# Reordering the logits' copy, the early gathers' operands and the early tile's transposes at the end of a fused attention and mixture-of-experts kernel

## The chip, the cores and the metric

The kernel runs on one core of a Trainium2 chip. The metric is the time of one execution on the device, in microseconds (us), as the median of several runs; lower is better. A core has five engines that work side by side, each through its own queue of instructions: TensorE (matrix products; PE in the profile, and PEld for its weight loads), VectorE (DVE), ScalarE (ACT), GpSimd (POOL) and SyncE (SP, which here only starts transfers). They meet through semaphores.

## What is computed

The reference is windowed attention, followed by a layer in which every token goes to one of eight experts. Shapes: 4 sequences of 768 tokens, 8 heads of width 64, 8 global columns, a local window of 96; 3072 tokens of width 512, experts 512 to 1024 to 512.

```python
scores = scale * np.matmul(q, k.transpose(0, 1, 3, 2)) + bias   # bias: -slope of the head * distance
scores = np.where(is_global | is_local, scores, -1000000000.0)
a = softmax(scores)
x = (a @ v) as tokens x 512

logits = x @ w_gate
expert_idx = np.argmax(logits, axis=1)
gate_w = softmax(logits)[own expert]
for e in range(E):
    xe = x[expert_idx == e]
    out[expert_idx == e] = gate_w * (np.maximum(xe @ w1[e], 0.0) @ w2[e])
```

## The kernel before, in words

**Attention.** A block is 128 queries of one sequence: 24 blocks, six in each of the four sequences. The loop in `banded` (L475 to L528) has steps n = 0 to 24, and in step n it works on several blocks at once, one stage each. All orders are those in which the code is written: the engines' queues are filled in program order (`manual_schedule`), nothing is moved by a scheduler. For the middle steps the order is:

- `scores(n)`: 32 products into two PSUM tiles `sp` (L360); VectorE adds the bias into two tiles `p` (L374, or L371 for a sequence's first block).
- `prep_q(n + 1)` and `prep_k(n + 1)`: transposes of the next raw q and k (L237), copied by ScalarE (L242); GpSimd puts the global columns into `ka` (L296, L297).
- `both(n - 1)`: VectorE adds the two halves of p of the block before into `pb` (L390), which gives the softmax sums.
- `exps(n, ...)`: the first of two exponentials on ScalarE (L381).
- `tokens(n - 2)`: TensorE transposes the router's row `rs` (L428) and the attention output `ot` (L431, into `px`); ScalarE copies the logits from PSUM to `part` (L436); VectorE forms the softmax denominators (L439, L441), the logits (L444, L447) and the scaled rows of x (L450, `xr`). For the last block of a sequence `choose` (L170 to L178) picks the expert, and in a later step `gates` (L181 to L190) forms the gate values.
- `values(n - 1)`: probabilities times v (L402) into `po`, copied by ScalarE into `ot` in two halves (L406); then the router's row into the PSUM tile `pr`: softmax sums (L413) and logits (L417), copied by ScalarE into `rs` (L420). `pr` has one buffer, which is free again once `part` is copied.
- the second exponential of block n, and `mix_v` (L281, GpSimd).

In steps 8, 14 and 20 a finished sequence is dispatched: `dispatch` counts places by small products (L198, L202), VectorE turns them into row numbers (L205 to L212), and in the steps that follow GpSimd scatters the rows of x to `xs_dram`, two blocks a step (L215).

**The early tile.** After three sequences the first 128 tokens of experts 0 and 1 are known. `early()` computes their row numbers by eight VectorE operations (L777 to L790) and gathers them (L732); `x_in_s(0)` transposes the first tile (L797), VectorE copies it (L798) and sets targets and gates (L799, L801). Its up-projection (`up_s`, L806) is the first work of the experts, and covers the dispatch of the fourth sequence. In step 24 the order is scores' sums `both(23)`, `values(23)`, `tokens(22)`, the early tile's `x_in_s(0)`, and after the loop `tokens(23)`.

**Experts.** `passes` then goes through all eight experts, by a scheme with seven products for eight (L978, L1040, L1049) and smaller forms for the rest of an expert's tokens; the change leaves it alone.

## Time and profile before

| | us |
|---|---|
| median of three runs (517.68, 518.26, 724.41) | 518.26 |
| profiled execution, span | 515.9 |
| attention up to the first up-projection (L806 in the chain) | 164.15 |
| TensorE busy | 498.8 |
| VectorE busy | 316.8 |
| ScalarE busy | 162.3 |
| GpSimd busy | 190.5 |

The granted TensorE clock is 0.997 over the span. A profile is one execution. Each row of a timeline gives the start, the busy time, the engine, the line and the operation with the tile written and the tiles read; in square brackets stands the idle time of the engine before it, and after the arrow who ended that wait. An engine that isn't the bottleneck may stand idle without cost, so the table's shares say little by themselves: what counts is which engine the others wait for in the stage that is changed. In the middle of attention the chain of waits goes through TensorE for step after step:

```profile
97.38 1.99 PE sp L360 x32
99.36 1.02 PE pt L237 x8
100.93 1.90 PE po L402 x32
103.25 0.52 PE pr L413 x10
104.35 1.99 PE sp L360 x32
```

One step takes some 7 us here, from scores to scores (97.38 to 104.35).

### The profile page before, as it was taken

To read this page: it belongs to the slowest core of one execution; us is meant where nothing else is said; L and a number is where in the kernel's file an instruction comes from. 1 tells how busy PE (TensorE), PEld (TensorE's weight loads), DVE (VectorE), ACT (ScalarE), POOL (GpSimd) and SP (SyncE) were. 2 spreads that over 40 slices of the span, in tenths; PEclk is the share of its full clock that TensorE was granted. 3 is DMA by queue.
4 is the path that set the end of the run, shared out by engine and by line. 5 is a ranking of instruction groups with operands and counts; after the bars stand their busy time and mean duration, and the time that the engine had idled before them with its cause. 6 is when DMAs were issued, how large, how long until landed. Compare 5 with 4: busy or idle time off the path is not lost.

```text
span 515.9 us, 12427 instructions
## 1 busy us (share of the span) xinstructions
PE 498.8 (97%) x5019; PEld 422.2 (82%) x5019; DVE 316.8 (61%) x666; ACT 162.3 (31%) x346; POOL 190.5 (37%) x285
## 2 busy tenths in 40 slices
PE   7999999999997999999999999999999999999994
PEld 4888888888886679679799788869969868896983
DVE  4787977977977646528599068128527705822741
ACT  4666656656652002113112012103102212211120
POOL 5431251351442573334384065034316305502503
PEclk9999999999999999999999999999999999999998
DMA  9999789789921321064191461047264108400101
GB/s 183 210 236 222 174 231 226 182 216 230 317 84 44 124 76 61 8 240 184 26 386 52 164 246 39 1 146 287 74 218 166 26 1 291 151 2 23 44 4 50
DMA packets 96334, 72.77 MB, mean 141 GB/s; under 512 B 79324, under 2 KB 79326, under 8 KB 96228
## 3 DMA queue, kind: packets, MB, share of 16 engines
q1 hardware_dynamic: 87808, 52.44, 36.8%
q0 software_dynamic: 7872, 19.01, 10.6%
q8 instruction: 54, 0.88, 0.8%
q14 instruction: 52, 0.43, 0.3%
q10 hardware_dynamic: 548, 0.02, 0.1%
HBM read 61.46 MB, written 14.73 MB: 148 GB/s over the span
## 4 chain that ended last, share of the span: by engine, by line
PE 86%; issue 5%; DVE 5%; DMA 1%; SPq 1%; POOL 1%; ACT 1%; POOLq 0%; ACTq 0%
PE u L978 18%; PE u L806 10%; PE d L1040 9%; PE sp L360 8%; PE d L1049 7%; PE u L816 7%; PE po L402 6%; PE pt L237 4%; PE d L816 3%; PE pr L413 3%; PE u L1147 3%; PE u L1122 3%; DVE p L374 2%; PE t L958 2%; PE px L431 1%
## 5 line engine op out<-in xcount | busy, mean ns | idle before, releaser
L1056 DVE TENSOR_TENSOR UV<-UV,d 128x512 f32<-128x512 f32 x8 | 5.5, 688 | 110.9 <-ACT yu L1150 81.3
L740 POOL DMA_INDIRECT out_dram<-ys,to_u x8 | 8.3, 1041 | 142.6 <-ACT yu L1150 87.6
L374 DVE TENSOR_TENSOR p<-sp,other 128x1024 f32<-128x1024 f32 x40 | 47.2, 1219 | 18.0 <-PE sp L360 13.8
L806 PEld LDWEIGHTS u<-xsT,w 128*128 128x128 f32 x448 | 50.9, 192 | 2.9 <-issue 2.0
L806 PE MATMUL u<-xsT,w 128*128 128x128 f32 x448 | 51.8, 276 | 0.9 <-DVE gates L801 0.9
L978 PE MATMUL u<-cx,c 128*128 128x128 f32 x384 | 48.1, 275 | 0.0
L381 ACT ACTIVATE p<-p 128x1024 f32<-128x1024 f32 (+1 forms) x48 | 47.2, 987 | 1.8 <-DVE p L374 1.6
L978 PEld LDWEIGHTS u<-cx,c 128*128 128x128 f32 x384 | 45.5, 192 | 0.0
L402 PE MATMUL po<-p,vt 128*64 128x128 f32 x704 | 43.7, 276 | 0.8 <-issue 0.5
L402 PEld LDWEIGHTS po<-p,vt 128*64 128x64 f32 x704 | 38.1, 137 | 5.0 <-issue 3.9
L978 PE MATMUL u<-xT,w 128*128 128x128 f32 x256 | 39.6, 277 | 0.0
L360 PE MATMUL sp<-qt,kt 64*128 64x128 f32 x448 | 37.8, 276 | 0.6 <-DVE kt L244 0.6
L816 PE MATMUL u<-w,huT 128*128 128x512 f32 x80 | 35.1, 592 | 0.0
L978 PEld LDWEIGHTS u<-xT,w 128*128 128x128 f32 x256 | 34.2, 192 | 1.0 <-issue 0.2
L360 PEld LDWEIGHTS sp<-qt,kt 64*128 64x128 f32 x448 | 31.0, 188 | 2.4 <-issue 1.2
L1040 PE MATMUL d<-c,ch 128*128 128x256 f32 x128 | 32.8, 379 | 0.0
L296 POOL COPY ka<-kt 128x384 f32<-128x384 f32 x16 | 10.1, 634 | 56.7 <-ACT kt L242 56.7
L215 POOL DMA_INDIRECT xs_dram<-xr,slot_i x24 | 24.4, 1016 | 16.2 <-DVE cnt L868 7.5
L816 PEld LDWEIGHTS u<-w,huT 128*128 128x128 f32 x80 | 15.2, 190 | 17.0 <-issue 16.7
L1005 ACT COPY uv<-u 128x256 f32<-128x256 f32 x32 | 11.9, 371 | 51.2 <-PE u L978 42.1
L390 DVE TENSOR_TENSOR pb<-p 128x512 f32<-128x512 f32 x40 | 27.6, 731 | 0.0
L1040 PEld LDWEIGHTS d<-c,ch 128*128 128x128 f32 x128 | 24.3, 190 | 3.3
(256 smaller groups left out, 1044.7 us busy)
## 6 DMA issues: line engine op xcount, KB each, us to landing
w<-in_moe_w_dram SPq DMA_DIRECT2D x24, 1024.0 KB
w<-in_moe_w_dram SPq DMA_DIRECT2D x16, 512.0 KB
raw_q<-in_q_dram SPq DMA_DIRECT2D x24, 256.0 KB
raw_k<-in_k_dram SPq DMA_DIRECT2D x24, 256.0 KB
vt<-in_v_dram SPq DMA_DIRECT2D x24, 256.0 KB
xs_dram<-xr,slot_i POOLq DMA_INDIRECT x24
xg<-xs_dram,grow POOLq DMA_INDIRECT x16
mu<-xs_dram,grow_e POOLq DMA_INDIRECT x16
```

The source lines that it names most:

```text
L215: d = nc.gpsimd.indirect_dma_start(out=xs_dram[:], out_offset=bass.IndirectOffsetOnAxis(ap=slot_i[:, u:u + 1], axis=0), in_=xr[:, u, :].bi ...
L237: nc.tensor.transpose(pt[:, m, :], src[:, 2 * m:2 * m + 2, :].rearrange("p a d -> p (a d)"), ident[:])
L360: nc.tensor.matmul(sp[:, a, j, t, :], lhsT=kt[r, m, :], rhs=qts[n][r, m, :], start=True, stop=True, skip_group_check=True)
L374: nc.vector.tensor_tensor(z, sc, bi, ALU.add)
L381: nc.scalar.activation(z, z, AF.Exp)
L390: nc.vector.tensor_tensor(t[:].rearrange("p a j c -> p (a j) c"), z[:, :, 0, :], z[:, :, 1, :], ALU.add)
L402: nc.tensor.matmul(po[D * a:D * a + D, m % 2, :], lhsT=vt[:, 2 * m + a, :], rhs=ps[n][m // 2][:, a, m % 2, t, :], start=(x == 0), stop=(x ...
L806: nc.tensor.matmul(ph[:, i, :], lhsT=self.w[e % 2][0][:, c, ts(half * HF + i, P)], rhs=xT[:, c, :], start=(c == 0), stop=(c == NDC - 1), s ...
L816: nc.tensor.matmul(py[:].rearrange("p a b -> p (a b)"), lhsT=h[:, f, :], rhs=self.w[e % 2][1][:, f, :], start=(f == 0), stop=(f == NFC - 1 ...
L978: nc.tensor.matmul(bank[:, r, :], lhsT=lhs(k), rhs=rhs(k), start=first, stop=True, skip_group_check=True)
L1040: nc.tensor.matmul(self.half(i, j), lhsT=lhs, rhs=rhs, start=(f == 0 and j == 0), stop=True, skip_group_check=True)
L1049: nc.tensor.matmul(self.half(i, j), lhsT=lhs(f), rhs=rhs(f), start=False, stop=True, skip_group_check=True)
```

## The change

Four lines of the loop move, and one function is cut in two.

- The first exponential of step n (for 1 < n < 24) goes behind `tokens(n - 2)`, so that ScalarE's queue has the copy of the logits (L436) ahead of it. For step 0 nothing changes.
- `early()` keeps its eight VectorE operations and goes from step 23 to step 22, behind the last scatters; its two gathers become `gather_early()`, in step 23.
- In step 24 the early tile's `x_in_s(0)` goes ahead of `tokens(22)`.

The aim is that VectorE gets the logits earlier in each step, that GpSimd need not wait for the gathers' operands, and that the first up-projection need not wait for work on the last tokens.

```diff
-            if n < N and n != 1:
-                exps(n, slice(0, 1 if 0 < n < N - 1 else 2))
             if n == 0:
+                exps(n, slice(0, 2))
                 biases(1, (0, 1, 2, 3), "act")
...
             if n == N:
                 rs[n - 1] = values(n - 1)
+                ex.x_in_s(0, ps_t.tile([P, NPAIR, P], F32, tag="t", name="pt"))
             if n >= 2:
                 tokens(n - 2, rs.pop(n - 2))
...
+            if 1 < n < N:
+                exps(n, slice(0, 1 if n < N - 1 else 2))
             if 0 < n < N:
                 rs[n - 1] = values(n - 1)
             if 0 < n < N - 1:
                 exps(n, slice(n != 1, 2))
-            if n == N:
-                ex.x_in_s(0, ps_t.tile([P, NPAIR, P], F32, tag="t", name="pt"))
             if n < N:
                 mix_v(n)
             if i == 2 and b == B - 1:
                 send()
+                ex.early()
             if i == 3 and b == B - 1:
-                ex.early()
+                ex.gather_early()
...
             nc.vector.tensor_scalar(self.inv_s[:, 0:NS], inv[:], float(2 ** 30), None, MUL)
-            for e in range(NS):
-                self.gather(self.xs[:, e, :], self.grow_s[:, e:e + 1])
             shape = [P, E, 5]
...
+        def gather_early(self):
+            for e in range(NS):
+                self.gather(self.xs[:, e, :], self.grow_s[:, e:e + 1])
```

## The prediction

> **What bounds the kernel now.** I read the busy shares first, then busy time by stage, the waits, the three timelines of the last attention steps, and the chain that ended last. The page's first two parts:

> ```profile
> PE 498.8 (97%) x5019; PEld 422.2 (82%) x5019; DVE 316.8 (61%) x666; ACT 162.3 (31%) x346; POOL 190.5 (37%) x285
> PE   7999999999997999999999999999999999999994
> ```

> TensorE is busy nearly all the time, with one dent: the thirteenth slice, around 155 us, the end of attention. A saving must be time in which TensorE stands still, and it must lie before about 164 us. The busy times by stage (columns: window, length, busy us of each engine) price that dent:

> ```profile
> 10.00:30.00 20.00, 19.94 (x306) 17.03 (x306) 14.86 (x33) 14.59 (x30) 11.86 (x27) 1.00 1.12 213
> 150.00:165.00 15.00, 11.09 (x166) 9.18 (x165) 11.01 (x32) 5.75 (x13) 4.93 (x6) 1.00 0.21 73
> 165.00:208.00 43.00, 42.78 (x296) 34.71 (x295) 27.52 (x83) 6.34 (x14) 22.88 (x28) 1.00 0.24 78
> ```

> From 150 to 165 us TensorE lacks 3.9 us; from 10 to 150 us it lacks 2.6 us in all (140 less the 137.4 us that the stages sum to). After 165 us it lacks next to nothing, so whatever is gained before stays gained. About 6.5 us is the most that this region can give. The waits between 149.5 and 164.2 us (engine and line, who was waited for, total, times, longest) say who takes it:

> ```profile
> POOL xs L732 <- DVE loc L788: 3.6, 1, 3.6
> PE pr L413 <- ACT part L436: 1.7, 1, 1.7
> PE u L806 <- DVE gates L801: 0.9, 1, 0.9
> PE pr L413 <- DVE pb L390: 0.7, 2, 0.5
> PE pt L797 <- DMA xs<-xs_dram,grow_s: 0.7, 1, 0.7
> ```

> The change speaks to each: L436 is the copied logits, L788 the last of the early operands, L797 the early tile's transposes. But a wait names who came last, not who comes next once it is gone. So the ScalarE timeline of step 23 and the chain (time, length, what):

> ```profile
> 153.45 2.19 ACT L381 ACTIVATE p<-p 128x1024 f32<-128x1024 f32 x2 [1.56 <-DVE p L374]
> 155.54 0.25 ACT L436 COPY part<-pr 128x128 f32<-128x128 f32 x1
> 155.69 0.65 ACT L406 COPY ot<-po 128x256 f32<-128x256 f32 x2
> ```

> ```profile
> 152.13 2.36 DVE p L374 x2
> 154.48 1.50 DVE pb L390 x2
> ...
> 157.47 0.08 DVE cnt_s L777
> ...
> 158.60 1.22 DVE pb L390 x2
> 159.82 0.04 issue
> 159.86 0.52 PE pr L413 x10
> ...
> 163.40 0.60 DVE xsT L798
> ```

> The part copy sits behind both exponentials, but so do the two ot copies, which the same router product needs at L417. And from 152 to 160 us the chain runs almost wholly on VectorE: score sums, pb sums, the tokens' rows, the eight operations of early() (157.4 to 158.6 us), then the pb sums of the last block. VectorE bounds this end, not the 1.7 us ScalarE wait.

> [...] the logits of step 23 are in PSUM at 151.82 us, yet their copy starts at 155.54. [...] the first early gather is an instruction of 1.09 us at 158.47, while TensorE's transposes of what it brings are let go at 162.06, 3.6 us after its start. [...] the pair of pb sums takes 1.28 us alone and 1.59 with GpSimd copies beside it (132.95 us). The change moves two gathers, so I allow 0.3 us for that.

> **The change, part by part.**

> (a) *Part copy ahead of the first exponential, in the steps whose router product waits for it.* In steps 7, 13 and 19 (52.03, 89.82, 128.14 us) TensorE waits 0.33 us for the copy, 1.0 in sum. The copy's input is there earlier: in step 19 its transpose is done by 126.4 (0.11 us at 126.24 in the chain), and ScalarE's kt copy ends at 126.99. So it runs at 126.9 instead of 127.83. But ScalarE does the same sum of work, so the ot copies still end at 128.6; L417's last four matmuls follow at 128.6 and the next scores at 128.85, against 129.03. I take 0.17 of each 0.33: 3 x 0.17 = **0.5 us** (bounds 0.2 and 1.0). In all other steps the copy is hidden behind TensorE's matmuls, and the exponential is 0.15 us later (the start-to-start of copy and next copy, 155.54 to 155.69), which the values of the *next* step do not feel: its product is wanted some 5 us later. Nothing there.

> (b) *The same, seen by VectorE.* In those three steps VectorE stands 1.40 us for the copy (den at 52.01, 89.80 and 128.12). With the copy ready at 127.15 the tokens' rows and the choice of expert end 0.97 us earlier, and the next score sums, now without any gap behind them at 130.68, start when their own scores allow: 128.85 + 1.17 (16 score matmuls) + 0.04 = 130.06, 0.62 earlier. Behind them in VectorE's queue are pb, tokens, dispatch and the next pair, an unbroken run up to 141.93 us, where TensorE waits for pb (0.40 us as matmul, 0.67 with its weight load, at 141.98). That run comes 0.62 earlier, 0.45 beyond what (a) already gave. In steps 9 and 15 the same wait is 0.29 and 0.34 us as a weight load (65.41, 103.25), of which I take 0.3 each. Sum 0.45 + 0.3 + 0.3 = **1.05 us** (bounds 0.4 and 2.0, the latter if the 0.3 us waits for ot in those steps shrink too).

> (c) *The 1.68 us wait of step 23.* Copy done at 152.1, so the product may start at 154.16. It can't: pb of block 22 ends its halves at about 155.1 and 155.99, and the ot copies now start at 155.54 instead of 155.69. Its matmuls end at 156.7, not 156.82: **0.1 us** (bounds 0 and 0.3). Two waits take the removed one's place.

> (d) *The eight operations of early() a step ahead.* In step 23 they occupy 157.38 to 158.52, 1.14 us of VectorE on the chain. In step 22 they fall between 150.57 (the end of the tokens' rows) and 152.13, where VectorE stands 1.56 us: hidden by that wait. So the last pb sums run 157.4 to 158.7, the last values end at about 158.65, and the router product ends at 159.6 instead of 160.71: 1.1 us, of which (c) gave 0.1. **1.0 us** (bounds 0.6 and 1.3).

> (e) *Gathers and the early tile.* The gathers' operands no longer hold GpSimd (3.63 us). They follow the vt copy (154.24 to 154.84) and start at 154.9; the same 3.6 us put the first tile in place at 158.5, over a microsecond before its transposes. These now follow the product at 159.6: 0.44 us of matmul, 0.2 to the copy, 0.60 copy, 0.15 for tos and gates: up-projection free at 161.2, and the tokens' transposes (0.55 + 0.55 us) fill TensorE meanwhile. Before: product end 160.71 to up-projection 164.15 is 3.44 us; after, 159.6 to 161.25 is 1.65. That is 1.8 us; it contains the gather wait (0.65) and the gates wait (0.91). Against it stands a debt: the last tokens' VectorE work follows the early tile's, and the expert choice ends at 161.1 + 1.57 (161.83 to 163.40) + 2.16 (164.05 to 166.21) = 164.85, while the dispatch comes up at 161.25 + 3.53 (164.15 to 167.68) = 164.8. The slack of 1.5 us (166.21 to 167.68) is used up. [...] **1.4 us** (bounds 0.5 and 2.0).

> After that GpSimd's scatters come 0.7 us nearer to TensorE than before; the tile they lead to was fetched from 181 us and is wanted at 189.97, so that is hidden.

> Sum: 0.5 + 1.05 + 0.1 + 1.0 + 1.4 = 4.05 us. 518.26 - 4.05 = 514.2 us, 0.8% less.

> **Rivals.** *Handed on:* VectorE or the engines' handshakes take back most of it. For it: some score sums wait until well after their scores (in step 22, at 145.12, 1.2 us after the first 16 matmuls), all in steps where scatters are under way, and gathers now move beside the last products. Then (a) at 0.2, (b) 0.4, (d) 0.6, (e) 0.5: 1.7, or 516.6 us. *All waits go:* every TensorE wait listed above and 1.0 in steps 7, 13, 19, 0.67 in 21 and 0.6 in 9 and 15 vanish: 1.7 + 0.9 + 0.7 + 0.7 + 1.0 + 0.67 + 0.6 = 6.3, or 512.0 us. Against it: the ot copies behind the exponentials. *Slower:* the copy ahead holds up the exponentials where TensorE waits for them next; 0.27 us (a whole copy) in each of some 20 steps costs 5.4 us, less (d), (e) at their low 1.1: 522.6 us. Against it: no TensorE wait in the trace names an exponential (L381).

> **How the numbers follow.** Forecast 0.60, handed on 0.25, all waits 0.10, slower 0.05. 514.2 us is the likeliest case. The range 511.8 to 517.2 us takes in the lower bounds of the terms' sum (1.7 us), the all-waits case, and leaves out the slower case and a little on each side. Over 2% would be 10.4 us either way, more than the 6.5 us that TensorE stands idle in this region and more than the slower case: faster 0.02, within 0.95, slower 0.03.

> **What would show it.** (a) L413 no longer waits for L436 anywhere; the 0.33 us waits shrink by half, with ot in their place. (b) At the step-21 dispatch L413 no longer waits for pb. (c) In step 23 L413 waits for pb instead. (d) L777 lies near 149 us and the last pb pair starts some 1.1 us sooner after the first. (e) GpSimd's gathers start before 155 us, and the first up-projection follows the last router product by under 2 us. I am wrong if the exponentials appear as a releaser of TensorE, if the dispatch waits for the expert choice by more than half a microsecond, or if the part after the first up-projection changes its length.

## The result and the profile after

The changed kernel takes 514.61 us in the median of six runs (514.32 to 514.86); the kernel before, run beside it, 517.68 in the median of five (517.00 to 518.26). A sixth run of the kernel before took 724.41 us and is left out. The ratio is **0.9941, with a 95% interval of 0.9927 to 0.9955**: a gain of 3.1 us, 0.6%. That is less than 2%, but well outside the scatter of the runs. The prediction said 514.2 us and a range of 511.8 to 517.2. The time came out closer than the gain: the sum said 4.05 us, and started from 518.26.

The first two parts of the page of the changed kernel, busy time by engine and the slices of TensorE:

```profile
PE 499.4 (97%) x5019; PEld 422.4 (82%) x5019; DVE 318.4 (62%) x666; ACT 162.3 (32%) x346; POOL 192.3 (38%) x285
PE   8999999999999999999999999999999999999994
```

The work is the same, and the dent in the thirteenth slice is gone. Busy times by stage, changed kernel, same columns as before:

```profile
10.00:150.00 140.00, 139.01 (x2162) 121.03 (x2159) 115.55 (x251) 89.11 (x185) 52.47 (x87) 1.00 0.87 216
150.00:165.00 15.00, 13.53 (x185) 11.94 (x182) 12.39 (x39) 6.17 (x14) 4.15 (x5) 1.00 0.20 62
```

TensorE lacked 3.9 us between 150 and 165 us; now it lacks 1.5. From 10 to 150 us it lacked 2.6 and now lacks 1.0. The windows stand still while the work moves, so the gain is better counted between events:

| from … to | before, us | after, us | gain, us |
|---|---|---|---|
| scores of block 1 … scores of block 23 | 10.98 … 149.51 | 10.58 … 148.22 | 0.89 |
| scores of block 23 … first up-projection | … 164.15 | … 160.10 | 2.76 |
| first up-projection … first product of the eight experts (L978, L981 after) | 30.13 long | 30.59 long | −0.46 |

The sum, 3.19 us, is close to the 3.1 us of the ratio. (The two profiled spans, 515.9 and 512.5 us, differ by 3.4: the scores of block 1 come 0.40 us earlier, and what follows the last row of the table is 0.2 us longer.) The waits of TensorE between 148 and 161 us, where there had been four, and further on one that the prediction did not have:

```profile
PE pr L413 <- DVE pb L390: 1.4, 1, 1.4
...
PE d L819 <- DVE loc L910: 0.6, 1, 0.6
```

The waits for the logits' copy, for the gates and for the gather are gone. The first remaining line is step 23, where pb has taken the place of the copy; the second is the down-projection, at 172.3 us. ScalarE's timeline of step 23, changed kernel (start, length, what):

```profile
151.16 0.27 ACT L436 COPY part<-pr 128x128 f32<-128x128 f32 x1 [0.54 <-PE px L431]
152.28 2.19 ACT L381 ACTIVATE p<-p 128x1024 f32<-128x1024 f32 x2 [0.86 <-DVE p L374]
154.38 0.63 ACT L406 COPY ot<-po 128x256 f32<-128x256 f32 x2
```

The copy is now ahead of both exponentials, but the two ot copies still follow them. The chain that ended last, from step 23 to the first up-projection (start, length, what):

```profile
150.97 2.36 DVE p L374 x2
153.32 1.38 DVE pb L390 x2
...
154.75 0.52 PE pr L413 x10
...
158.51 0.59 PE pt L800 x4
...
160.19 3.76 PE u L809 x32
```

Before, the chain ran on VectorE up to 159.82 us, through the eight operations of early() and a second pair of pb sums. Now it leaves VectorE at 154.70 and stays on TensorE, with the early tile's transposes (L800) directly behind the last router product.

One thing about these two profiles has to be known for what follows. In both, VectorE starts the score sums of step 23 late: 2.62 us after the scores before the change, 2.75 after it. In seven of the eight profiles from two other chips, used in the experiments, it is 1.21 us (1.52 in the eighth), and there the changed kernel has no wait for pb in step 23 at all: the router product follows the value products at once, and TensorE waits 0.62 us for the early gather instead. There is no profile of the kernel before from those two chips, so how its time divides there is not known.

### The profile page after: what moved, and what is told of

It is laid out like the page before. It is cut to its first block, busy times and chain, and to the rows that moved or that the text cites. A ratio compares the mean times of both kernels' runs of the same rounds, so it can differ in the third digit from the quotient of the medians.

```text
span 512.5 us, 12427 instructions
## 1 busy us (share of the span) xinstructions
PE 499.4 (97%) x5019; PEld 422.4 (82%) x5019; DVE 318.4 (62%) x666; ACT 162.3 (32%) x346; POOL 192.3 (38%) x285
## 4 chain that ended last, share of the span: by engine, by line
PE 85%; DVE 7%; issue 5%; DMA 1%; SPq 1%; POOL 1%; POOLq 0%; ACT 0%; DVEq 0%
PE u L981 18%; PE u L809 10%; PE d L1043 10%; PE sp L360 8%; PE d L1052 7%; PE u L819 7%; PE po L402 6%; PE pt L237 3%; DVE p L374 3%; PE pr L413 3%; PE u L1150 3%; PE u L1125 3%; PE d L819 2%; DVE pb L390 2%; PE t L961 2%
## 5 line engine op out<-in xcount | busy, mean ns | idle before, releaser
L374 DVE TENSOR_TENSOR p<-sp,other 128x1024 f32<-128x1024 f32 x40 | 47.1, 1218 | 19.2 <-PE sp L360 14.2
L981 PE MATMUL u<-cx,c 128*128 128x128 f32 x384 | 48.1, 275 | 0.0
L381 ACT ACTIVATE p<-p 128x1024 f32<-128x1024 f32 (+1 forms) x48 | 47.7, 997 | 1.1 <-DVE p L374 0.9
L981 PEld LDWEIGHTS u<-cx,c 128*128 128x128 f32 x384 | 45.5, 192 | 0.0
L981 PE MATMUL u<-xT,w 128*128 128x128 f32 x256 | 39.6, 277 | 0.0
L981 PEld LDWEIGHTS u<-xT,w 128*128 128x128 f32 x256 | 34.2, 192 | 1.1 <-DVE cx L974 0.2
L390 DVE TENSOR_TENSOR pb<-p 128x512 f32<-128x512 f32 x40 | 28.3, 748 | 0.0
## 6 DMA issues: line engine op xcount, KB each, us to landing
w<-in_moe_w_dram SPq DMA_DIRECT2D x16, 512.0 KB
```

The lines of the kernel that those rows point to most:

```text
L374: nc.vector.tensor_tensor(z, sc, bi, ALU.add)
L381: nc.scalar.activation(z, z, AF.Exp)
L390: nc.vector.tensor_tensor(t[:].rearrange("p a j c -> p (a j) c"), z[:, :, 0, :], z[:, :, 1, :], ALU.add)
L981: nc.tensor.matmul(bank[:, r, :], lhsT=lhs(k), rhs=rhs(k), start=first, stop=True, skip_group_check=True)
```

## The experiments

My theory: the gain is made at the end of attention, by gathers that start early and a tile that no longer stands behind the last tokens; the first move, of the logits' copy, gives a little in the steps around each dispatch. Rivals: each move brings its own share whatever the others do; the gain is all in the first move; the ot copies hide more than I had thought. Three groups of runs, each on a chip of its own, with the kernel before beside it: its medians were 517.69, 514.21 and 514.33 us. The first group is the single moves and the run without the first move; the third starts with "The changed kernel again". So I compare ratios, or kernels of one group. "Over the changed kernel" on the first two chips means against 0.9941 of the kernel before there; on the third the changed kernel ran itself. A step's length is counted from its scores to the next block's.

### One move alone

**The logits' copy alone** (the first exponential behind `tokens(n - 2)`, the rest as before):

```diff
-            if n < N and n != 1:
-                exps(n, slice(0, 1 if 0 < n < N - 1 else 2))
             if n == 0:
+                exps(n, slice(0, 2))
...
+            if 1 < n < N:
+                exps(n, slice(0, 1 if n < N - 1 else 2))
```

> Only the first move: the logits' copy ahead of the exponentials; early operands, gathers and the early tile stay as in the kernel before. My theory (terms a, b, c): VectorE gets the logits earlier, the wait for pb in the dispatch steps goes, and in step 23 pb takes the copy's place: 0.9 us less than before (517.0), most of it in steps 9 to 21, and no gain between the scores of block 23 and the first up-projection. Rival (ScalarE wait is the bound at the end): step 23 gives its 1.7 us too, 2.6 us less (515.3). Rival (all handed on): no change (517.9).

517.13 us, ratio 0.9989 (0.9982 to 0.9995): 0.56 us gained. Steps 9, 15 and 21 take 6.34, 6.53 and 6.75 us, where the kernel before takes 6.94, 6.97 and 7.12. From the scores of block 23 to the first up-projection it takes 14.66 us, as before (14.64): nothing at the end. Both are as my theory had it.

**The operands alone** (`ex.early()` in step 22, `ex.gather_early()` in step 23, the gathers cut out of `early`):

```diff
+                ex.early()
             if i == 3 and b == B - 1:
-                ex.early()
+                ex.gather_early()
```

> Only the second move: the eight operations of early() in step 22, the gathers alone in step 23. My theory (term d and the gather wait of e): VectorE's chain in step 23 is 1.1 us shorter and the gather's 0.65 us wait goes, but the early tile's copy stays behind tokens(22) on VectorE: 1.4 us less than before (516.5). Rival (the operands only cost GpSimd idle time): 0.65 us or less (517.3).

516.62 us, ratio 0.9975 (0.9967 to 0.9984): 1.3 us. The end takes 13.20 us, 1.44 shorter. TensorE now waits 1.2 us for the gates, 0.9 before: the gathers land early, but the tile stands behind the last tokens.

**The early tile alone** (`x_in_s(0)` ahead of `tokens(22)`):

```diff
             if n == N:
                 rs[n - 1] = values(n - 1)
+                ex.x_in_s(0, ps_t.tile([P, NPAIR, P], F32, tag="t", name="pt"))
...
-            if n == N:
-                ex.x_in_s(0, ps_t.tile([P, NPAIR, P], F32, tag="t", name="pt"))
```

> Only the third move: the early tile's transposes ahead of tokens(22). My theory: the gather still lands at about 162 us, so TensorE waits there with the tokens' transposes behind it; up-projection 0.4 us earlier, but the last tokens' VectorE work and the expert table later, so that TensorE waits longer for the table's forms: between 0.5 us less and 0.5 us more, 517.9 within noise. Rival (the gates wait of 0.91 us is removed by this move alone): 0.9 us less (517.0).

517.8 us, ratio 1.0001 (0.9991 to 1.0011). TensorE's waits between 146 and 168 us in this kernel:

```profile
PE pr L413 <- ACT part L436: 1.8, 1, 1.8
PE pt L796 <- DMA xs<-xs_dram,grow_s: 1.3, 1, 1.3
```

The gates' wait is gone, and the wait for the gather has grown from 0.7 to 1.3 us: one took most of the other's place. The first up-projection still comes 0.49 us earlier (14.15 us after the scores of block 23), but from there to the first product of the eight experts it takes 30.60 us, not 30.13: TensorE stands 0.66 us in the down-projection, where it stood 0.22. So what was won was lost there, as the theory in that text had it.

The three moves alone give 0.56 + 1.3 + 0 = 1.9 us, together 3.1. Each of these is known to 0.3 to 0.7 us only, but the traces say the same: between the scores of block 23 and the first up-projection the single moves take off 0, 1.44 and 0.49 us, together 2.76. So they need one another.

### One move undone

**Without the first move** (changed kernel, first exponential back in its old place):

```diff
+            if n < N and n != 1:
+                exps(n, slice(0, 1 if 0 < n < N - 1 else 2))
             if n == 0:
-                exps(n, slice(0, 2))
```

> The second and third move without the first. My theory: the end of attention gains as in the changed kernel, 2.7 us from the scores of block 23 to the first up-projection, less 0.4 us at the table's forms: 2.3 us less than before (515.6), 1.0 us over the changed kernel. If the first move does nothing: as the changed kernel (514.6). If the first move is needed for the end (the 1.7 us wait comes back): 1.7 us or more over the changed kernel (516.3).

516.29 us, ratio 0.9969 (0.9958 to 0.9981): 1.45 us over the changed kernel by the ratios, 1.65 by the medians (0.9941 of 517.69 us is 514.64). That lies between the 1.0 of my theory and the 1.7 of the last case, and it came by a way that none of them named. TensorE's timeline at the end (start, length, what, idle time before it):

```profile
155.31 0.70 PE L413 MATMUL pr<-pb,one_in 128*32 128x128 f32 x16 [1.82 <-DVE pb L390]
...
156.20 3.55 PE L402 MATMUL po<-p,vt 128*64 128x128 f32 x32
```

The last 32 value products take 3.55 us; in this kernel's other steps they take 1.97. The busy times by stage show why; the column ahead of the DMA share is the granted clock:

```profile
153.00:156.00 3.00, 1.18 (x34) 0.94 (x30) 2.93 (x6) 2.73 (x5) 1.90 (x3) 1.00 0.01 3
...
157.00:158.00 1.00, 1.00 (x12) 1.00 (x11) 1.00 (x3) 0.27 (x1) 0.98 (x2) 0.50 0.79 173
```

In the three microseconds up to 156 TensorE worked for 1.18; then the clock fell (0.69, 0.50, 0.50 and 0.61 in the four microseconds from 156 to 160; it is full again behind them), which cost 3.55 − 1.97 = 1.6 us. The profiles of the kernels before and after hold the full clock there, with gaps of 1.68 and 1.37 us.

The fall did not come in every run of this kernel. The mean granted clock of a run is on record: of the eight, five have 0.994, as the profiled one (516.22 to 517.38 us), and three 0.997 to 0.998 (515.22, 515.31 and 516.32 us). All profiles with no fall have 0.996 to 0.999. The three lie, by their median, 0.7 us over the changed kernel; the rest of the 1.65 us goes with the fall.

**Without the second move** (`ex.early()` whole, with its gathers, in step 23):

```diff
-                ex.early()
             if i == 3 and b == B - 1:
-                ex.gather_early()
+                ex.early()
```

> The changed kernel with the second move undone: early() whole in step 23 again. My theory (term d and the gather): its eight operations lie on VectorE's chain again (1.1 us) and the gather lands when the early tile is wanted, so the first up-projection comes 2 to 2.5 us later than in the changed kernel: 516.9. Rival (the first move alone carries the end): within 0.5 us of the changed kernel (515).

513.17 us, ratio 0.9982 (0.9972 to 0.9991): 0.0041 of 514.21, 2.1 us over the changed kernel. The end takes 12.56 us against 10.79 in the changed kernel on the third chip (1.8 longer), and TensorE waits 1.3 us for the early tile's gather again, the same as with the early tile alone. Three of the ten runs, at 513.87 to 514.00 us, have the mean clock of 0.994 that goes with a fall; the profiled one has none.

**Without the third move** (`x_in_s(0)` back behind `values`, the rest changed):

```diff
-                ex.x_in_s(0, ps_t.tile([P, NPAIR, P], F32, tag="t", name="pt"))
...
+            if n == N:
+                ex.x_in_s(0, ps_t.tile([P, NPAIR, P], F32, tag="t", name="pt"))
```

> The changed kernel with the third move undone: the early tile behind tokens(22) again. My theory (term e without the gather): its copy waits behind 1.5 us of tokens(22) on VectorE, so the up-projection is 1.2 us later, but TensorE does not wait longer for the expert table's forms (0.4 us): 0.8 us over the changed kernel, 515.4. Rival (additive with the single moves, where the tile alone gave nothing): as the changed kernel, 514.6. Rival (gates wait of 0.91 and idle TensorE bring the slower clock back, as in the run without the first move): 516.4.

511.66 us, ratio 0.9948 (0.9934 to 0.9961): 0.36 us over the changed kernel, half of what I expected, and by the intervals not to be told from it. In the profiles the first up-projection is indeed 0.75 us later (11.53 us after the scores of block 23, against 10.79), with 1.3 us of waiting for the gates. But further on:

```profile
PE d L820 <- issue: 0.2, 1, 0.2
```

The down-projection stands only 0.2 us, where the changed kernel's stands 0.65, and the stretch from the first up-projection to the eight experts takes 30.12 us, not 30.59. So of the 0.75 us that the third move wins ahead of the up-projection 0.47 is lost here. The run with the forms' table read later comes back to it.

### What holds the rest

**The ot copies ahead of the first exponential**, in steps 2 to 22 (changed kernel otherwise):

```diff
-        def values(n):
+        def values(n, mid=None):
...
+            if mid:
+                mid()
...
-            if 1 < n < N:
-                exps(n, slice(0, 1 if n < N - 1 else 2))
+            if n == N - 1:
+                exps(n, slice(0, 2))
             if 0 < n < N:
-                rs[n - 1] = values(n - 1)
+                rs[n - 1] = values(n - 1, (lambda: exps(n, slice(0, 1))) if 1 < n < N - 1 else None)
```

`mid` runs between the ot copies and the router product.

> The changed kernel with the two copies of the attention output also ahead of the first exponential (steps 2 to 22). My theory (term c and the failed term a: the ot copies took the place of the logits' copy): the 0.3 us wait for ot in steps 7, 13 and 19 goes, and those in steps 9 and 15: 1.0 us under the changed kernel, 513.6. Rival (VectorE's pb sums come last in those steps): no change, 514.6. Rival (the exponential now comes too late for the next values): slower, 516 or more.

511.11 us, ratio 0.9938 (0.9924 to 0.9952), 0.2 us under the changed kernel by the ratios, and not to be told from it, as the first rival has it. The steps tell more. Step 19 of the kernel before, from the second ot copy to the next scores (start, length, what):

```profile
127.97 0.67 ACT L406 COPY ot<-po 128x256 f32<-128x256 f32 x2
...
129.03 0.49 PE L360 MATMUL sp<-qt,ka 64*128 64x128 f32 x4
```

The same of the changed kernel:

```profile
127.04 0.66 ACT L406 COPY ot<-po 128x256 f32<-128x256 f32 x2
...
127.47 0.42 PEld L417 LDWEIGHTS pr<-ot,gate_w 128*32 128x32 f32 x8 [0.29 <-ACT ot L406]
...
128.09 0.49 PE L360 MATMUL sp<-qt,ka 64*128 64x128 f32 x4
```

and of this kernel (the lines of the file are two further on):

```profile
125.28 0.75 ACT L406 COPY ot<-po 128x256 f32<-128x256 f32 x2 [0.33 <-PE po L402]
...
125.90 0.33 PEld L419 LDWEIGHTS pr<-ot,gate_w 128*32 128x32 f32 x8
```

With the ot copies ahead, L419 has no wait, and steps 7, 13 and 19 fall from 5.87 to 5.47 us each. So it was the ot copies that held them at 5.87 after the logits' copy had been taken away. But steps 9, 15 and 21 go from 6.34, 6.53 and 6.75 us (changed kernel, third chip) to 6.67, 6.67 and 7.06. Step 21 of this kernel shows who holds it:

```profile
139.31 0.52 PE L415 MATMUL pr<-pb,one_in 128*32 128x128 f32 x10 [0.40 <-DVE pb L390]
```

No exponential is named there. From the logits of step 19 to the pb sums of step 21 VectorE works with no gap over 0.1 us and ends them 18.3 us after the scores of step 19, as in the changed kernel (18.4). TensorE now gets there 0.4 us earlier, and waits. So of the 1.2 us that was won 0.8 is handed back, by VectorE's unbroken run.

**The forms' table read later** (changed kernel, one line moved):

```diff
         ex.down_s(0, ex.hsT, 0, ex.d[0])
-        ex.load_forms()
         ex.down_s(0, ex.hsT, 1, ex.d[0])
+        ex.load_forms()
```

`load_forms` reads a form for each expert from a small table into the engines' registers, TensorE's too; VectorE writes the table in `table()`.

> The changed kernel with TensorE's reading of the expert forms one group of eight products later, behind the first early tile's second half. My theory (the debt of the third move: VectorE's table comes nearer to TensorE, which waits for it at 172.3 us): the gap of 0.77 us in the down products goes: 513.9. Rival (the reading itself costs TensorE's queue a microsecond wherever it stands): no change, 514.6.

510.3 us, ratio 0.9923 (0.991 to 0.9937): 0.9 us under the changed kernel by the ratios, whose intervals overlap. In the profile the first up-projection comes 29.70 us ahead of the first product of the eight experts, where the changed kernel has 30.59: the same 0.9 us, and the rival fails. The timelines around 170 us (start, length, what, idle time before it): first the kernel before, then the changed one with the table's last write, then this one:

```profile
175.88 2.38 PE L816 MATMUL d<-w,hsT 128*128 128x512 f32 x5 [0.22 <-issue]
```

```profile
170.89 0.17 DVE L898 TENSOR_SCALAR form<-k_i 128x8 int32<-128x8 int32 x1
...
172.30 1.96 PE L819 MATMUL d<-w,hsT 128*128 128x512 f32 x4 [0.65 <-DVE loc L910]
```

```profile
165.03 7.03 PE L819 MATMUL d<-w,hsT 128*128 128x512 f32 x16
```

Half of the sixteen products lie ahead of the read and half behind it. In the first two kernels TensorE stands between the halves, 0.22 and 0.65 us; with the read eight products later the sixteen products are one run. The wait's name, L910, was only the VectorE instruction that ended last before it; what TensorE's queue waited for is the read of the table, whose last write, at L898, ends 1.2 us before the next product. All the profiles agree: with the third move and the read in its old place the gap is 0.53 to 0.66 us (eight kernels), without the third move 0.21 to 0.22 (four).

**The changed kernel again**, beside the next three:

> The changed kernel once more, beside the three that follow. Expected: 0.994 of the kernel before. In steps 7, 13 and 19 a period of 5.87 us from scores to scores, as before the change; at the table's forms a wait of 0.65 us. If the late score sums of steps 10, 11 and 22 belong to the change: periods of 6.8 to 7.1 us there; if to the chip: on one where they are missing 6.34 us, as in the runs e5 to e8.

511.25 us, ratio 0.9941 (0.9928 to 0.9955), the same ratio as at first. The end takes 10.79 us, and steps 10, 11 and 22 take 6.34 us each, where the first profile of this kernel has 6.81, 7.13 and 6.78; the wait at the forms is 0.65 us in both. So the late score sums go with the chip. The changed order has a part in where they fall: in the first group step 10 is long only in the kernels with the first move (6.81 and 6.84 us), step 16 only in those without it (6.91 to 6.97; 6.50 in the one with the clock's fall).

**Both together**, ot copies ahead and the table read later:

> The changed kernel with both: ot copies ahead of the first exponential, and the forms read one group later. My theory: 0.4 us in each of steps 7, 13 and 19, of which steps 9, 15 and 21 take back 0.8 because VectorE's pb sums come last there, and 0.65 us at the forms: 1.0 us under the changed kernel run beside it, 0.992 of the kernel before. Rival (the two are the same slack seen twice): 0.65 us under it.

510.26 us, ratio 0.9919 (0.9905 to 0.9932): 1.0 us under the changed kernel beside it and 4.1 under the kernel before. The runs alone do not tell 1.0 from the rival's 0.65. But both savings are in the profile, each in its place: the sixteen products are one run, and steps 7, 13 and 19 take 5.47 us. It is the fastest of the versions tried on that chip.

**The scatters spread**, one a step instead of two in the first two sequences, to see whether they make some score sums late:

```diff
-            for _ in range(min(2, len(sends))):
+            for _ in range(min(2 if n >= 20 else 1, len(sends))):
```

> The changed kernel with the scatters of the first two dispatched sequences one a step over six steps, instead of two a step over three. Theory (score sums start late while scatters are in flight): on a chip where steps 10, 11 show it, the lateness shrinks there and shows in later steps; the total within 0.5 us of the changed kernel. Rival (lateness has nothing to do with scatters): the same periods in steps 10 and 11. On a chip without the lateness: no change beyond 0.3 us.

522.13 us, ratio 1.0158 (1.0144 to 1.0172): slower, and for a reason that I had missed. VectorE's wait:

```profile
DVE xr L450 <- DMA xs_dram<-xr,slot_i: 10.4, 2, 6.8
```

The rows of the next sequence overwrite a buffer that is still being scattered, so step 15 takes 10.16 and step 21 13.58 us. On this chip no score sums were late in the first place, so the run says nothing on its question.

**Idle products in the gap, without the first move**: the kernel without the first move, with six matmuls that add nothing to the result ahead of step 23's router product, to keep the clock up:

```diff
+        def fill():
+            t = ps_s.tile([P, 2, 2, 2, P], F32, tag="s", name="fill")
+            spot = t[:, 0].rearrange("p j t c -> p (j t c)")
+            for _ in range(6):
+                nc.tensor.matmul(spot, lhsT=idle[:, 0:P], rhs=idle[:], start=True, stop=True,
+                                 skip_group_check=True)
...
-                rs[n - 1] = values(n - 1)
+                rs[n - 1] = values(n - 1, fill if n == N - 1 else None)
```

> The second and third move without the first, with six idle products on zeros (about 1.3 us at full clock) in TensorE's gap of step 23, so that it does not stand still there. They add no work to the result. Theory (the 1.8 us gap brought the half clock that cost 1.6 us in the run without the first move): no stretch of clock under 1.0 around 157 us, and 0.7 us over the changed kernel run beside it. Rival (the slower values of block 23 had another cause): 1.7 us over it. Rival (the idle products push the router product back): 1 us or more over it with full clock.

512.34 us, ratio 0.9964 (0.995 to 0.9977): 1.1 us over the changed kernel beside it. The clock is full around 157 us, and no run has a mean under 0.996, so this is the worth of the first move with no fall of the clock in it. 0.9 of it is in steps 9, 15 and 21 (6.67, 6.72, 7.12 us without the move; 6.34, 6.53, 6.75 with it), nothing in steps 7, 13 and 19 (5.87 in both). The end is 0.35 us longer (11.14 against 10.79), so the idle products can account for about that much at most, not for the 1 us of the last rival. Whether they kept the clock up is not shown: the kernel without them did not run on this chip.

## Why the prediction was right, and where it was not

The direction, the time and the place were right: 3.1 us measured against 4.05 summed, most of it at the end of attention. The gain was a quarter too large; that the time still came within 0.4 us of 514.2 is luck, since the sum started from 518.26 and the kernel before took 517.68 beside the changed one. By its own steps:

**(a) Steps 7, 13, 19: predicted 0.5, measured 0.** These steps take 5.87 us each, before and after. The wait for L436 is gone, as said, but the ot copies took all of it, not half. The step that failed is "L417's last four matmuls follow at 128.6 and the next scores at 128.85": it lets the scores start 0.25 us after the ot copies. In both traces it is 0.39 (128.64 to 129.03 before, 127.70 to 128.09 after). So the next scores had followed the ot copies all along; the wait for the logits' copy ran beside theirs, and taking it away could give nothing. The run with the ot copies ahead shows it: without them in the way 0.4 us falls from each step.

**(b) The pb waits of steps 9, 15, 21: predicted 1.05, measured 0.9 to 1.4.** The mechanism is as forecast. VectorE stands 0.45 us for the copy in step 19, not 1.40, and the score sums of step 20 start 7.08 us after the scores of step 19, not 7.52: 0.44 earlier, where the prediction had 0.45 beyond what (a) gives. The wait of 0.40 us at the step-21 dispatch is gone from the list. By the idle-product run the three steps give 0.9 us; by the two profiles of before and after 0.61 + 0.44 + 0.37 = 1.4. In those two profiles, though, steps 10, 11, 16, 17 and 22 together grew by 0.56 us (33.12 to 33.68), since score sums on VectorE started about 1 us late, with scatters in flight. So the net of the loop, 0.89 us, is not a clean measure of (a) and (b). What makes the sums late was not found.

**(c), (d) and (e): predicted 2.5, measured 2.76 less 0.46.** From the scores of block 23 to its value products it takes 7.31 us before and after: (c), predicted 0.1, gave 0. pb is the wait that follows in step 23, as said, but only in the profiles with late score sums. From the start of the value products to the end of the last router product it is 0.92 us shorter, where (d) had 1.0: the eight operations lie at 149.19 to 150.51 us, ahead of the score sums, and the pair of last pb sums starts 3.08 us after the first instead of 4.12. From there to the up-projection (e) had 1.8 us; it is 1.84. The first gather is issued at 153.77, the last router product ends at 158.5 and the up-projection starts at 160.10: 1.6 us, where 1.65 was predicted and 3.44 had been. The choice of expert, at 163.5, is just ahead of the dispatch at 163.78, as worked out (the sum in the text gives 164.83, not 164.85; nothing hangs on it): the slack is used up but nothing waits.

**What (e) had wrong.** It looked for the cost of the earlier up-projection in the dispatch and in the scatters ("hidden"), and not at who else reads what VectorE makes after it. With the up-projection ahead of the last tokens VectorE starts the dispatch 4.71 us after the up-projection's start, not 4.00, so the table of forms is written 10.96 us after it, not 10.68, and TensorE waits for it in the middle of the down-projection: 0.65 us instead of 0.22. With that the stretch is 0.46 us longer, the last row of the first table; by the prediction's own test ("or the part after the first up-projection changes its length") this step was wrong. The run without the third move (0.2 us) and the run with the table read later (none) show it from both sides. That (e) came out at 1.84 − 0.46 = 1.4 us, as predicted, is luck: the prediction had taken off about as much (1.8 to 1.4) as an allowance.

**What the sum did not have.** The moves were added as if each had its worth. Alone they gave 1.9 us. The tile ahead gives nothing until its gather lands early; with the early gather it gives some 0.3 us (0.36 by the runs, whose intervals overlap, 0.28 by the profiles). The first move gives 0.56 alone and 0.7 to 1.1 with the others and a full clock, on different chips.

**The rivals.** "Handed on" (516.6) was right on (a) but not on the end. "All waits go" (512.0) failed on the ot copies, as the text held against it. "Slower" (522.6) failed on the time. Its sign, an exponential as a releaser of TensorE, appears once in the changed kernel, at a weight load of step 23 (1.6 us), but the matmul that needs these weights waits for pb.

## What to carry to other kernels

A wait that is taken away leaves the next one that ends near it: list every input of the waiting instruction with its time, add what lies between an input's end and the work that follows (0.39 us here, not 0.25), and price the edit by the second latest. When work moves ahead of other work, follow what is now late to *all* its readers, also to a register read in another engine's queue (a wait of 0.65 us here). Moves at one place should be priced as a set, since a tile that comes early is worth nothing before its data does.

## What the runs showed of the hardware

```profile
142.00:143.00 1.00, 0.00 (x0) 0.00 (x0) 0.00 (x0) 0.00 (x0) 0.00 (x0) 0.55 0.11 41
...
149.00:150.00 1.00, 1.00 (x28) 0.83 (x28) 0.93 (x4) 0.42 (x2) 0.84 (x2) 1.00 0.37 140
```

  In the first of these microseconds the clock has a mean of 0.55. From 143 to 148 it is 0.50, from 148 to 149 it is 0.54, and in the last it is 1.00 again, between 4 and 5 us after TensorE had taken up work at 144.06.
- From the write of a small table in SBUF to the next product behind TensorE's read of it passed 1.0 us before (174.83 to 175.88) and 1.2 after (171.06 to 172.30). Each time TensorE stood in between, 0.22 and 0.65 us.
- The kernel before differed by 0.7% between chips (517.69 against 514.21 us), more than the change brings. The ratio of the changed kernel to it did not differ: 0.9941 in both comparisons.
